# One row block ahead of the last filter load, and the gate products moved behind the kv transforms

## The chip, the cores and the metric

The kernel runs on one core of one Trainium2 chip. A time is the device time of one execution in microseconds (us). The engines are TensorE (PE; its weight loads are listed apart as PEld), VectorE (DVE), ScalarE (ACT), GpSimd (POOL) and SyncE (SP), which issues most of the DMAs. Each engine works through its own instructions in the order in which they were written.

## The reference

Two mixers share one input `x = A_q` (2048 rows, D = 640, bf16), and a gate per row mixes them:

```python
g = sigmoid((x * gate_w).sum(-1))
kv = causal_shift_conv(k, shift_k) * v            # 4 taps
a = x * (causal_long_conv(kv, ssm_k) + kv * ssm_D) # by FFT, length 2S
h = layernorm(x)
b = (gelu(h^T @ w1 + b1) @ w2 + b2)^T             # MLP over the 2048 rows, F = 1536
return g * a + (1 - g) * b
```

## The kernel before, in words

**The convolution.** The FFT is done as matrix products with a table of sines and cosines (`FTB`), after a split of the rows by position modulo 4. The filter `ssm_k` is loaded in five pieces: three for its first half (`SSM0`, line 765) and two for its second (`SSM1`). Each 128-column block is turned by TensorE (`transp`, line 838; evacuated by ScalarE as `wT`), then transformed (`fwd`, `fwd_even`, evacuated as `C`), then combined on VectorE (`mixing`, line 889). K is shifted by small matmuls against `KF` (`kv`, line 1003), multiplied by v, and transformed in the same way; the second half of that product is `kv1`, which lies at `E_base`. `KT`, the turned k, lies there too and is dead by then. VectorE multiplies the transformed parts (`cross`, line 1178; `product`, line 1138), with some sums left to accumulating DMAs from the POOL queue, recombines them (`invmix`), and TensorE transforms back (`inverse`, line 1209).

**The MLP.** The rows (`X`, four blocks of 512 rows, `x_load`, line 737) get their statistics on VectorE (`ln_tile`, line 913), a power on GpSimd (`ln_scale`), and are normalised in place (`ln_apply`). The first MLP product is called m1 (twelve column tiles `ft`, Gelu on ScalarE into `GT`), the second m2 (sixteen tiles). Both are cut into groups of eight matmuls.

**The gate.** The row sum of `X * gate_w` is taken from the normalised rows: VectorE writes a product of two tiles into a buffer `gq`, and ScalarE sums each tile by a copy with an accumulator (`gsum`, lines 1078 to 1085; sixteen of them in `gacc`). `gws` is the sum of the gate's weights. From these `gth`, then a tanh, then `gg`, `omg` and `c2` follow (lines 1087 to 1093). `gq` has two buffers, in space that is later `q_hi`.

**What sets the order.** Every operation is first recorded, with its engine, a duration from a formula, a priority (its place in the program, or a given one: `prio=0` first, MLP groups last) and what it depends on by overlapping memory. Then a list scheduler (`_Sched.run`, line 384) plays this on a clock of its own: each engine takes, whenever it is free, the ready operation with the lowest priority number. A DMA is booked as its bytes over `rate` (365 unless given) behind all earlier DMAs, and lands 2.0 later. At most three convolution tiles and two MLP tiles are in PSUM at once. The instructions are written out in the order that comes out of this. So an edit of a rate, which changes no instruction, can change the order of all engines; an edit of an address changes what has to wait for what.

The MLP groups have the largest priority numbers: in the planner's list they stand wherever TensorE would otherwise have nothing to do.

The lines of the gate and of the loads:

```python
SSM0 = ((0, 1), (1, 3), (3, 5))
...
for a, b in SSM0:
    ssm_load(0, a, b)
for hk in range(4):
    x_load(hk)
```

Of the kernel before, what the change touches and what calls it, by code (L numbers as in the profile page):

```python
# [9 lines left out]
BF16 = mybir.dt.bfloat16  # L10
F32 = mybir.dt.float32
I32 = mybir.dt.int32
ACT = mybir.ActivationFunctionType
# [497 lines left out]
def _build(nc, A_q, A_k, A_v, A_shift_k, A_ssm_k, A_ssm_D, B_x, B_w1, B_b1, B_w2, B_b2, gate_w, out):  # L511
    Bsz, S, D = A_q.shape
# [9 lines left out]
    with ExitStack() as es:  # L522
# [4 lines left out]
        for i in range(4):  # L527
            h = es.enter_context(nc.psum_tensor(f"pp{i}", [128, 1024], F32))
# [7 lines left out]
        def alloc(name, shape, dtype, at=None):  # L536
            size = mybir.dt.size(dtype)
            for s_ in shape[1:]:
                size *= s_
            if at is None:  # L540
                off = cur[0]
                cur[0] = (off + size + 63) // 64 * 64
            else:
                off = at
            assert off % 4 == 0 and off + size <= top, f"SBUF overflow {name}: {off}+{size} > {top}"
            h = nc.alloc_sbuf_tensor_at(name, list(shape), dtype, offset=off)
            T.reg_sbuf(h, off)
# [21 lines left out]
        gacc = alloc("gacc", [128, 16], F32)  # L569
        gws = alloc("gws", [128, 1], F32)  # L570
# [7 lines left out]
        X = alloc("X", [128, 4, 4, D], BF16)  # L578
# [4 lines left out]
        E_base = cur[0]  # L583
# [2 lines left out]
        dif = alloc("dif", [128, 128], I32, at=base_of(SS) + 64 + 1024)  # L586
        dif2 = alloc("dif2", [128, 32], I32, at=base_of(SS) + 64 + 1536)
        KT = [alloc(f"KT{i}", [128, NG, KTW], BF16) for i in range(2)]
        gq = [alloc(f"gq{i}", [128, 2, D], BF16, at=base_of(Drow) + 5120 + 2560 * i) for i in range(2)]
        ssm = alloc("ssm", [128, ND, S], BF16, at=base_of(C[3]))  # L590
        wT = alloc("wT", [128, 4, 4, D], BF16, at=base_of(C[2]))
        vkv0 = alloc("vkv0", [128, 2, 4, D], BF16, at=base_of(C[3]))
# [25 lines left out]
        def act_dur(n, nap=0):  # L618
            return n / 1200.0 + 0.09 + 0.05 * nap

        def tt(eng, o, a, b, op, mode=2, prio=None, xr=()):
            n = n_of(o)
            d = dve_dur(n, mode) if eng == "DVE" else n / 600.0 + 0.17
            rd = [a, b] + list(xr)
            o_ = SC.add(eng, d, lambda s: T.op(eng, lambda e: e.tensor_tensor(o, a, b, op), rd, [o]),  # L625
                        rd, [o], prio=prio, name="tt")
            o_.lock = True
            return o_
# [23 lines left out]
        def act(o, i, func, bias=None, scale=None, acc=None, vt=None, prio=None, name="act"):  # L652
            kw = {}
            rr = []
            nap = 0
            for k_, v_ in (("bias", bias), ("scale", scale)):
                if v_ is not None:
                    kw[k_] = v_
                    if isinstance(v_, bass.AP):
                        rr.append(v_)  # L660
                        nap += 1
            ww = [o]
            if acc is not None:
                kw["accum_out"] = acc
                ww.append(acc)

            def emit(s):
                src = i(s) if vt is not None else i
                return T.op("ACT", lambda e: e.activation(o, src, func, **kw), rr + [src], ww)  # L669
            return SC.add("ACT", act_dur(n_of(o), nap), emit, rr if vt is not None else rr + [i], ww, prio=prio, vt=vt, name=name)  # L670
# [16 lines left out]
        def mms(vt, items, prio=None, name="mm"):  # L687
            dur = sum(max(n_of(r) / 2400.0 + 0.0025, 0.056) for _, _, r, _, _ in items)
            rd = []
            for _, l, r, _, _ in items:  # L690
                rd += [l, r]

            def emit(s):
                fv = T.cnt["PE"] + 1
                for k_, (o, l, r, st, sp) in enumerate(items):
                    T.mm(o(s), l, r, st, sp, fv, k_ == len(items) - 1)
            return SC.add("PE", dur, emit, rd, [], prio=prio, vt=vt, name=name)
# [4 lines left out]
        def dma(o, i, nbytes, stream="SP", prio=None, sem=None, rate=365.0, chain=False, **kw):  # L702
            if sem is None:
                sem = f"d{ndma[0]}"
                ndma[0] += 1
            if sem not in T.dma_sems:
                T.add_dma_sem(sem, es.enter_context(nc.semaphore(f"s_{sem}")))
            rd = [i] + ([o] if kw.get("accum") else [])
            o_ = SC.add(stream, nbytes / rate / 1000.0, lambda s: T.dma({"QA": "ACT"}.get(stream, stream), o, i, sem, **kw), rd, [o], prio=prio, lat=-1.0, name="dma")
            if chain:  # L710
                if last[0] is not None:
                    o_.after.add(last[0])
                last[0] = o_
# [11 lines left out]
        def chk(ci):  # L725
            return lambda s: s[:, ci * 512:ci * 512 + 320]

        def ssm_load(h, a, b):
            dma(ssm[:, a:b, 1024 * h:1024 * h + 1024], dr(A_ssm_k, 128 * S * a + 1024 * h, [[S, 128], [128 * S, b - a], [1, 1024]]), 128 * (b - a) * 2048, chain=True)

        def row8(t, hk):
            return dr(t, (1024 * (hk // 2) + 4 * (hk % 2)) * D, [[8 * D, 128], [1, 4 * D]])
# [2 lines left out]
            return 16 + 128 * (1 - hk % 2)  # L735

        def x_load(hk):
            dma(X[:, hk, :, :], dr(A_q, 512 * hk * D, [[4 * D, 128], [1, 4 * D]]), 128 * 5120, chain=True)

        def w1_load(c, hk):  # L740
            dma(ring[c % 2][:, 4 * hk:4 * hk + 4, :], dr(B_w1, 512 * hk * F + 512 * c, [[4 * F, 128], [F, 4], [1, 512]]), 128 * 4096, chain=True)
# [20 lines left out]
        def small(o, i, nbytes, stream, **kw):  # L762
            dma(o, i, nbytes, stream=stream, **kw)

        SSM0 = ((0, 1), (1, 3), (3, 5))
        SSM1 = ((0, 2), (2, 5))
        small(Drow[:, :], dr(A_ssm_D, 0, [[0, 1], [1, D]]), 1280, "QA")
        small(rows[0:20, 0, 0:128], dr(A_shift_k, 0, [[128, 20], [1, 128]]), 5120, "QA")
        for a, b in SSM0:
            ssm_load(0, a, b)  # L770
        for hk in range(4):
            x_load(hk)
        small(rows[0:4, 1, :], dr(B_b2, 0, [[512, 4], [1, 512]]), 4096, "SP", chain=True)
        small(rows[0:12, 2, 0:128], dr(B_b1, 0, [[128, 12], [1, 128]]), 3072, "SP", chain=True)
        for a, b in SSM1:
            ssm_load(1, a, b)
# [280 lines left out]
        for ft in range(FT):  # L1057
            if ft == 4:
                for hk in range(4):
                    w1_load(2, hk)  # L1060
            if ft == 9:
                for p in range(4):
                    gil = act(V(FTB, 1024 * p, [[1, 2], [256, 4], [2, 128]]), V(GTB, 1024 * p, [[512, 2], [128, 4], [1, 128]]), ACT.Copy, prio=10 ** 5, name="gil")
                    gil.after.add(g_)
            vt = _VT("mlp")
            r = ring[(ft // 4) % 2]
            col = 128 * (ft % 4)
            for hk in range(4):
                items = []
                for p in range(4):  # L1070
                    for ci in range(2):
                        items.append((chk(ci), r[:, 4 * hk + p, col:col + 128], X[:, hk, p, 320 * ci:320 * ci + 320],
                                      hk == 0 and p == 0, hk == 3 and p == 3))
                mms(vt, items, prio=10 ** 6 + 4 * ft + hk, name="m1")
            g_ = act(GT[:, ft, :].rearrange("p (a b) -> p a b", a=2), two, ACT.Gelu_apprx_tanh, bias=cc[:, 16 + ft:17 + ft], vt=vt, prio=0, name="gelu")
            if ft == 0:
                act(gq[1][:, 0, :], gwb[:, :], ACT.Copy, acc=gws[:, :], name="gws").after.add(g_)
            if ft in (1, 3, 5, 7):
                hk = ft // 2
                for a in range(2):  # L1080
                    gb = gq[a]
                    tt("DVE", gb[:, :, :], X[:, hk, 2 * a:2 * a + 2, :], V(gwb, 0, [[0, 2], [1, D]]), ALU.mult)
                    for b in range(2):
                        t = 4 * hk + 2 * a + b
                        act(gb[:, b, :], gb[:, b, :], ACT.Copy, acc=gacc[:, t:t + 1], name="gsum")

        tt("DVE", gth[:, :], sd[:, :], gacc[:, :], ALU.mult, mode=1, prio=0)
        ts("DVE", gpre[:, :], mv[:, :, 0], gws[:, 0:1], None, ALU.mult, mode=1)
# [221 lines left out]
```

## Time and profile before

| | us |
|---|---|
| median of 4 runs | 184.74 (184.35 to 185.58) |
| the profiled execution | 184.35 |
| its span, first to last instruction | 182.6 |
| PE busy | 172.7 |
| DVE busy | 171.7 |
| ACT busy | 117.4 |
| POOL busy | 39.1 |

The profile is one execution. A line of the timeline gives start, duration, engine, line, operation, what it writes and reads, and in brackets how long the engine was idle before it and what released it. In the list of waits the columns are the total, how many times, and the longest. Almost all operations pass through helpers, so most of them share a line (L625 is every elementwise product of VectorE, L669 every ScalarE activation, L293 every matmul); tile names tell them apart. Tile numbers are left out: `C` is four arrays, and `ssm`, `wT`, `vkv` and `SS` are other names with spaces of their own. The clock of TensorE was 1.0 throughout.

### The profile page before, as it was taken

What the parts mean: (1) busy time and instruction counts of PE and PEld (TensorE: products, weight loads), DVE (VectorE), ACT (ScalarE), POOL (GpSimd) and SP (SyncE); (2) the same over time, 40 slices, a digit from 0 to 9 for tenths busy, and PEclk for the clock granted to TensorE, in tenths of its full rate; (3) what the DMA queues carried; (4) which work ended last, traced back from release to release, by engine and by line L of the source; (5) the groups of instructions that cost most, each with busy time, mean ns of one, the idle gap of its engine ahead of it and who ended that gap; (6) DMA issues with size and microseconds to landing.
All of it is one profiled execution on the core that took longest, in us unless ns stands there. A gap on an engine that the chain in (4) does not pass through costs nothing.

```text
span 182.6 us, 3317 instructions
## 1 busy us (share of the span) xinstructions
PE 172.7 (95%) x1373; PEld 127.0 (70%) x1374; DVE 171.7 (94%) x203; ACT 117.4 (64%) x176; POOL 39.1 (21%) x42
## 2 busy tenths in 40 slices
PE   7978998889999999999999999999999999999991
PEld 2644584676777777776777778888888886678670
DVE  7799895999999999999998999999999979999975
ACT  5799988899989978159999931321313213761660
POOL 4069604000000055000510210303443000054000
PEclk9999999999999999999999999999999999999999
DMA  5999999999999989997499969799999997369584
GB/s 156 407 408 370 390 251 238 316 418 199 193 259 280 193 169 242 229 230 168 138 245 260 251 152 353 142 233 344 202 194 273 220 209 204 132 104 232 95 286 148
DMA packets 38542, 43.51 MB, mean 238 GB/s; under 512 B 15867, under 2 KB 31360, under 8 KB 38528
## 3 DMA queue, kind: packets, MB, share of 16 engines
q1 hardware_dynamic: 33296, 32.16, 59.2%
q0 software_dynamic: 5200, 11.14, 34.2%
q8 instruction: 11, 0.18, 0.4%
q10 hardware_dynamic: 32, 0.01, 0.0%
q14 instruction: 3, 0.02, 0.0%
HBM read 25.87 MB, written 2.62 MB: 156 GB/s over the span
## 4 chain that ended last, share of the span: by engine, by line
PE 38%; DVE 30%; ACT 18%; DMA 9%; issue 3%; DVEq 0%; SPq 0%
PE pp L293 38%; DVE C L625 21%; DMA C<-SS 7%; ACT C L669 5%; ACT gq L669 5%; DVE tm L625 4%; DMA ssm<-in_A_ssm_k_dram 3%; ACT FTB L669 2%; DVE q_hi L625 2%; ACT wT L669 2%; ACT GT L669 2%; DVE gq L625 1%; DVE SS L625 1%; ACT L669 1%; ACT ksh L669 1%
## 5 line engine op out<-in xcount | busy, mean ns | idle before, releaser
L625 DVE TENSOR_TENSOR C<-C 128x2560 bf16<-128x2560 bf16 (+2 forms) x37 | 54.7, 1522 | 1.7 <-DMA C<-SS 1.2
L293 PE MATMUL pp<-X,ring 128*128 128x320 bf16 x384 | 55.1, 299 | 0.0
L293 PE MATMUL pp<-GT,W 128*128 128x320 bf16 x384 | 52.8, 299 | 0.0
L293 PEld LDWEIGHTS pp<-GT,W 128*128 128x128 bf16 x384 | 43.4, 113 | 8.8 <-ACT cgb L669 0.2
L293 PEld LDWEIGHTS pp<-X,ring 128*128 128x128 bf16 x384 | 37.3, 98 | 14.4
L669 ACT ACTIVATE C<-pp 128x640 bf16<-128x640 f32 x64 | 40.1, 725 | 5.0 <-PE pp L293 5.0
L669 ACT ACTIVATE O<-pp,c,omg 128x640 bf16<-128x640 f32 x15 | 13.3, 886 | 33.8 <-PE pp L293 33.8
L262 POOL DMA_DIRECT2D C<-C x8 | 10.9, 1609 | 46.7 <-DVE C L625 46.3
L293 PE MATMUL pp<-wT,FTB 128*128 128x320 bf16 x112 | 17.8, 301 | 1.6 <-ACT C L669 1.4
L669 ACT ACTIVATE cgb<-pp,gg 128x640 bf16<-128x640 f32 x16 | 12.7, 794 | 8.9 <-PE pp L293 8.9
L293 PEld LDWEIGHTS pp<-wT,FTB 128*128 128x128 bf16 x112 | 9.5, 97 | 8.8 <-ACT C L669 5.2
L669 ACT ACTIVATE GT<-pp,cc 128x640 bf16<-128x640 f32 x12 | 9.4, 786 | 8.3 <-PE pp L293 8.2
L919 DVE BATCH_NORM_STATS2 stats<-X 128x6 f32<-128x320 bf16 x32 | 13.7, 465 | 0.9 <-DMA X<-in_A_q_dram 0.9
L625 DVE TENSOR_TENSOR tm<-C,C 128x2560 bf16<-128x2560 bf16 (+1 forms) x7 | 14.3, 2057 | 0.0
L293 PE MATMUL pp<-C,FTB 128*128 128x320 bf16 x96 | 13.6, 299 | 0.5 <-DVE C L625 0.5
L262 POOL DMA_DIRECT2D C<-q_hi x6 | 5.9, 978 | 31.2 <-DVE C L625 16.2
L293 PEld LDWEIGHTS pp<-C,FTB 128*128 128x128 bf16 x96 | 9.0, 98 | 4.7 <-issue 0.7
L669 ACT ACTIVATE gq<-gq 128x640 bf16<-128x640 bf16 x16 | 11.6, 732 | 0.3 <-DVE gq L625 0.3
L625 DVE TENSOR_TENSOR SS<-C 128x2560 bf16<-128x2560 bf16 x8 | 11.7, 1487 | 0.1
L625 DVE TENSOR_TENSOR C<-tm 128x2560 bf16<-128x2560 bf16 (+1 forms) x9 | 10.6, 1192 | 0.1
L669 ACT ACTIVATE wT<-pp 128x1024 bf16<-128x1024 f32 x10 | 9.5, 1034 | 1.2 <-PE pp L293 1.2
L293 PE MATMUL pp<-KF,KT 128*128 128x128 bf16 (+1 forms) x160 | 9.0, 213 | 1.2 <-ACT GT L669 1.1
(73 smaller groups left out, 186.9 us busy)
## 6 DMA issues: line engine op xcount, KB each, us to landing
ring<-in_B_w_dram SPq DMA_DIRECT2D x12, 512.0 KB, 11.0
W<-in_B_w_dram SPq DMA_DIRECT2D x12, 512.0 KB, 7.2
C<-C POOLq DMA_DIRECT2D x8, 640.0 KB, 11.8
X<-in_A_q_dram SPq DMA_DIRECT2D x4, 640.0 KB, 8.2
kn<-in_A_k_dram SPq DMA_DIRECT2D x4, 640.0 KB, 9.4
out_dram<-O SPq DMA_DIRECT2D x7, 320.0 KB, 3.0
C<-SS POOLq DMA_DIRECT2D x3, 640.0 KB, 12.3
ssm<-in_A_ssm_k_dram SPq DMA_DIRECT2D x3, 512.0 KB, 5.5
```

The source lines that it names most:

```text
L262: ins = engobj.dma_start(out_ap, in_ap, accum_op=ALU.add, max_dma_last_dim=2560)
L293: ins = self.nc.tensor.matmul(ps_ap, lhsT=lhsT, rhs=rhs, start=start, stop=stop, skip_group_check=True)
L625: o_ = SC.add(eng, d, lambda s: T.op(eng, lambda e: e.tensor_tensor(o, a, b, op), rd, [o]), rd, [o], prio=prio, name="tt")
L669: return T.op("ACT", lambda e: e.activation(o, src, func, **kw), rr + [src], ww)
L919: ops.append(SC.add("DVE", 0.38, (lambda o, i: lambda s: T.op("DVE", lambda e: e.bn_stats(o, i), [i], [o]))(o, i), [i], [o]))
```

## The change

First, the loads: the first X block is issued between the second and the third filter piece, where before all three filter pieces went first. The booked rates are other ones: 262 for the first filter piece, 195 for the next two, 385 for the second half, 410 for X.

Second, the gate: the products use four buffers at `E_base`, the space of `kv1` (and of the dead `KT`), where before there were two in the later `q_hi`. So they have to wait until the transforms of `kv1` have read it. The scratch row of `gws` gets its own name, `gqd`. All eight products are recorded at `ft == 0`, where before two each were recorded at `ft` 1, 3, 5 and 7; in the program they stand behind the transforms of kv and ahead of `cross`, as before.

```diff
-        gq = [alloc(f"gq{i}", [128, 2, D], BF16, at=base_of(Drow) + 5120 + 2560 * i) for i in range(2)]
+        gqd = alloc("gqd", [128, D], BF16, at=base_of(Drow) + 5120)
+        gq = [alloc(f"gq{i}", [128, 2, D], BF16, at=E_base + 2560 * i) for i in range(4)]
...
         def ssm_load(h, a, b):
-            dma(ssm[...], dr(A_ssm_k, ...), 128 * (b - a) * 2048, chain=True)
+            dma(ssm[...], dr(A_ssm_k, ...), 128 * (b - a) * 2048, chain=True, rate=(262.0 if a == 0 else 195.0) if h == 0 else 385.0)
...
         def x_load(hk):
-            dma(X[:, hk, :, :], dr(A_q, ...), 128 * 5120, chain=True)
+            dma(X[:, hk, :, :], dr(A_q, ...), 128 * 5120, chain=True, rate=410.0)
...
-        for a, b in SSM0:
+        for a, b in SSM0[:2]:
             ssm_load(0, a, b)
-        for hk in range(4):
+        x_load(0)
+        ssm_load(0, *SSM0[2])
+        for hk in range(1, 4):
             x_load(hk)
...
             if ft == 0:
-                act(gq[1][:, 0, :], gwb[:, :], ACT.Copy, acc=gws[:, :], name="gws").after.add(g_)
-            if ft in (1, 3, 5, 7):
-                hk = ft // 2
-                for a in range(2):
-                    gb = gq[a]
+                act(gqd[:, :], gwb[:, :], ACT.Copy, acc=gws[:, :], name="gws").after.add(g_)
+            if ft == 0:
+                for t in range(0, 16, 2):
+                    hk, a = t // 4, t // 2 % 2
+                    gb = gq[t // 2 % 4]
                     tt("DVE", gb[:, :, :], X[:, hk, 2 * a:2 * a + 2, :], V(gwb, 0, [[0, 2], [1, D]]), ALU.mult)
                     for b in range(2):
-                        t = 4 * hk + 2 * a + b
-                        act(gb[:, b, :], gb[:, b, :], ACT.Copy, acc=gacc[:, t:t + 1], name="gsum")
+                        act(gb[:, b, :], gb[:, b, :], ACT.Copy, acc=gacc[:, t + b:t + b + 1], name="gsum")
```

More of the change, by code (lines that the diff above doesn't have):

```diff
@@ L728, in ssm_load @@
         def ssm_load(h, a, b):
-            dma(ssm[:, a:b, 1024 * h:1024 * h + 1024], dr(A_ssm_k, 128 * S * a + 1024 * h, [[S, 128], [128 * S, b - a], [1, 1024]]), 128 * (b - a) * 2048, chain=True)
+            dma(ssm[:, a:b, 1024 * h:1024 * h + 1024], dr(A_ssm_k, 128 * S * a + 1024 * h, [[S, 128], [128 * S, b - a], [1, 1024]]), 128 * (b - a) * 2048, chain=True, rate=(262.0 if a == 0 else 195.0) if h == 0 else 385.0)
         def row8(t, hk):
@@ L737, in x_load @@
         def x_load(hk):
-            dma(X[:, hk, :, :], dr(A_q, 512 * hk * D, [[4 * D, 128], [1, 4 * D]]), 128 * 5120, chain=True)
+            dma(X[:, hk, :, :], dr(A_q, 512 * hk * D, [[4 * D, 128], [1, 4 * D]]), 128 * 5120, chain=True, rate=410.0)
         def w1_load(c, hk):
```

## The prediction

> **What bounds the kernel now.** I read the page's busy shares first, then the table of stretches, then the waits, then the timeline at each wait.
>
> ```profile
> PE 172.7 (95%) x1373; PEld 127.0 (70%) x1374; DVE 171.7 (94%) x203; ACT 117.4 (64%) x176; POOL 39.1 (21%) x42
> ```
>
> TensorE and VectorE are both nearly full: of 182.6 us PE is idle for 9.9, DVE for 10.9. An edit that removes no instruction can only move these idle pieces. The table of stretches says where they lie (busy time out of the stretch's length: PE, PEld, DVE, ACT, POOL).
>
> ```profile
> 28.00:30.00 2.00, 1.98 (x15) 1.18 (x13) 0.92 (x4) 1.12 (x2) 0.87 (x2) 1.00 1.18 245
> 30.00:32.00 2.00, 1.15 (x6) 0.44 (x7) 0.94 (x3) 2.00 (x4) 1.24 (x2) 1.00 1.14 215
> 36.00:38.50 2.50, 1.35 (x24) 1.20 (x24) 2.43 (x4) 2.49 (x5) 0.00 (x0) 1.00 1.00 414
> 38.50:80.00 41.50, 41.45 (x378) 30.57 (x379) 41.00 (x29) 32.87 (x50) 5.10 (x4) 1.00 1.05 233
> 80.00:153.00 73.00, 72.76 (x536) 57.05 (x533) 70.85 (x61) 37.13 (x64) 14.40 (x13) 1.00 0.96 226
> ```
>
> From 38.5 to 153 PE loses 0.05 + 0.24 us: the MLP matmuls fill every hole. What PE loses, it loses before 38.5 (0.85 at 30 to 32, 1.15 at 36 to 38.5) and after 178. DVE loses 0.5 + 2.15 us there, and its waits name it:
>
> ```profile
> DVE X L640 <- POOL rstd L625: 2.7, 2, 2.1
> DVE C L625 <- DMA C<-SS: 1.2, 1, 1.2
> DVE stats L919 <- DMA X<-in_A_q_dram: 0.9, 1, 0.9
> DVE gth L625 <- ACT gq L669: 0.5, 1, 0.5
> ```
>
> The last two are what the diff touches. The row that ties both engines together is on PE's timeline:
>
> ```profile
> 153.22 0.97 PE L293 MATMUL pp<-C,FTB 128*128 128x320 bf16 x6 [0.46 <-DVE C L625]
> ```
>
> At 153.22 the inverse transforms start, and PE had to wait 0.46 us for VectorE. So VectorE's chain, from the second normalisation at 31.07 to 153.2, sets the end; PE is only 0.46 us behind. After 153.22 PE is full until 178.5. A microsecond gained on PE alone before 153 is given back there; one lost on DVE is lost in full.
>
> [...] the trace has 1.28 us at 34.90, ahead of the first Gelu. The planner's costs know no such load. [...] The trace has 0.72 for one gsum, but with its accumulator read 0.72 from start to start; the planner books 640/1200 + 0.09 = 0.62. [...] 410 to 430 GB/s from 6 to 11 us.
>
> **Part 1, the loads.** Nothing is added; one 640 KB X block goes ahead of the last 512 KB filter load. From the issues and their times to landing: ssm (1,3) is in at 5.89 (PE's wait ends there); ssm (3,5) is issued at 1.64 and takes 5.5, so 7.2; X block 0 is issued at 2.20 and takes 6.6, so 8.8. At about 400 GB/s the 640 KB take 1.6 us: X block 0 lands at 7.5, the filter piece at 8.8, all later blocks as before.
> VectorE: it waited 0.89 us until 8.80 for X. In the new order it is free at 7.91 and X is there, so the statistics, and the last angle product behind which POOL's four KF products queue (8.13 us, first start 10.77), begin 0.89 earlier. rstd, the first normalised rows (20.93) and, after the same 2.11 us wait for POOL, the second eight (31.07) come at 20.04 and 30.18. Gain so far: 0.89.
> ScalarE: the new rates change the planner's order. It now believes that the second and third filter pieces land later (5.79 and 10.09 on its clock, 4.26 and 5.71 before). By its priorities two sines then go ahead of wT evacuations: the third sine before wT1 (a near tie on its clock, 6.583 against 6.589), the fourth before wT3. The trace had those sines at 11.91 and 16.59, 1.03 us each, with PE waiting. The work is the same. wT4 then ends at about 13.2 instead of 11.9, but the 16 C evacuations (0.6 each) have no sine among them. I get their end at 23.6 to 24.5 against 23.58, the spread being whether PE, which now meets the first MLP group inside this phase, waits for X (about 0.45 us) in the middle of it. Cost on PE at this point: +0.1 to +0.9. After it there is one more MLP group already done or in reach, and the holes at 30 to 32 and 36 to 38.5 (2.0 us) are partly filled: I take 0.5 gained. Net on PE to 38.5: -0.4, from -1.2 to +0.6.
> The catch: VectorE after 31.07 does a few products and then needs the last C evacuation of the second filter half. In the trace that evacuation stands behind the table load and the first Gelu (34.90 + 1.28, Gelu to 36.99, C to 37.59), and DVE resumed at 37.61. These ScalarE times hang on the filter chain, not on X. With VectorE at 36.7 there, it waits for nearly the same 37.5. So of the 0.89 us I keep 0.1 as likeliest, up to 0.89 if the planner, seeing that evacuation late, puts another product in between. I take -0.3.
> The K transposes move too: the planner has K landing 1.8 us later, so the two DVE permutes at 23.07 and 24.92 go behind the last normalised rows, some 0.8 us later; their transposes on SP (23.92, 6.92 us for both), and the v and k loads queued behind them at 30.89, shift by as much. KT landed at 32.7 for a first use at 35.02, v (5.2 us) at 36.1 for 39.93: hidden. Without that cover it would be 0.8 us on VectorE.
>
> **Part 2, the gate products.** Eight products on DVE (0.73 from start to start) and sixteen gsums on ACT (0.72) stay. They now write the space of kv1, so the first must wait for the last kv1 matmul (84.68 + 0.71 = 85.4); in the trace two products ran at 81.30 and 84.84, ahead of that. VectorE will not idle: the first cross product (1.40) is ready and takes the slots of those two (1.47). The first gate product comes at about 85.5, just when kv1 is dead; two C[3] differences (2.80) go ahead of the next, so three more products come from 88.4 to 90.6 and, by the four buffers, the last near 95. Cost on DVE so far: nothing, covered by the cross products, 16 pieces of 0.73 to 1.40; if these were not ready, 1.4 us.
> The sum over the rows (gth) then waits for ScalarE. From the second gate product (ends about 89.9) 14 gsums and two Gelus (0.68) remain: 14 x 0.72 + 2 x 0.68 + 0.1 = 11.5, so 101.4. By the planner's 0.62 they would be 14 x 0.1 = 1.4 us sooner, and it puts gth at the first slot after that; VectorE reaches gth at about 100.2 and stands for 1.2 us, against 0.53 before. Bounds: the slot's rounding, up to one 1.40 us product, may swallow all of it (-0.5 against before) or it may be 1.9 (+1.4). I take +0.7. Behind gth on DVE stand the cross products, the C[3] sums, and so all up to 153. The gates' own end has slack: c2 at 103.44 for a first user at 111.57.
>
> **Sum.** VectorE at 153.2: -0.3 + 0.7 = +0.4; PE arrives 0.4 earlier and waits longer for it. The rest is unchanged. The profiled execution took 184.35 (span 182.6 and 1.75 around it), so 184.75; the median of the runs shown lies 0.39 above the profiled one, so 185.1 in its terms. A measurement of this kernel can tell about 0.5% (0.92 us) from no change, so this counts as the same.
>
> **Rivals.**
> Faster: VectorE keeps its lead of 0.89 at 37.6 and gth waits no longer than 0.53. For it: the hole before gth has room for 1.40 us of rounding, and PE has 2.0 us of early idle to give. Against: ScalarE's table load ends where it ended. Then -0.9 at 153.2, and the 0.46 us wait shrinks with it: 183.8, at best 183.3.
> Slower: one MLP group changes sides. The planner's list has the inverse's first input at 149.52 on its clock, between group ends at 149.20 and 150.28. I get PE's useful work 0.19 late on that clock, as the W transforms start 2.7 later and most of it is caught up by 39. From a lag of 0.33 on, one MLP group less runs before the inverse and one more after, where PE has no hole: 8 matmuls, 1.09 us from start to start. With VectorE's +0.4: 186.2. For it: 0.14 us decides. Against: the same rounding can give a group back.
> The change does not do what it says: the filter piece behind X lands much later than 8.8 (the new rates would have it past 10), ScalarE starves before wT3, and the filter chain, with everything hung on it at 37.6, is 0.5 to 1 us late: 185.8.
>
> **How the numbers follow.** Forecast 0.45 (its own range 184.1 to 185.6), faster 0.22, a group moved 0.23, the late filter piece 0.10. The last two together make slower, 0.33. For 8 in 10 the range takes in the faster case down to 183.7 and the moved group with the longer gth wait up to 186.7.
>
> **What would show it.** DVE's wait for X at 8.8 gone, statistics from 7.9; a DVE wait for ACT C near 37; gate products after 85; gth's wait for gq over 1 us; PE's wait for DVE at the first inverse matmul grown from 0.46 to about 1.2. I am wrong if that wait shrinks, if gth waits under 0.5, or if the MLP matmuls left after the inverse starts (56 now) are another number.

## The result, and the profile after

The kernel after has a median of 185.95 us (183.73 to 187.82, 43 runs); the kernel before, measured beside it, 185.46 (183.79 to 187.46, 64 runs). The ratio is 0.9984, with a 95% interval of 0.9963 to 1.0005: by the bound of 0.5%, no change. In terms of the 184.74 of the front page this is 184.4. The medians are over all runs, while the ratio leaves out those over 1.5% above the fastest of their kernel (19 of 43 after, 6 of 64 before), which is why the two don't agree in sign.

The profiled execution took 185.93 us, its span is 183.8, so it is 1.2 us longer than that of the kernel before. Its loads came late, as the experiments will show. First the page's busy shares and its row of TensorE's clock in 40 slices:

```profile
PE 174.6 (95%) x1373; PEld 128.9 (70%) x1374; DVE 171.8 (93%) x203; ACT 117.6 (64%) x176; POOL 43.5 (24%) x42
...
PEclk9958999999999999999999999999999999999999
```

The instruction counts are the same, VectorE's work too (171.8 against 171.7). TensorE is busy 1.9 us longer for the same 1373 matmuls, and the clock row has a dip in the third and fourth slices, 9 to 18 us, that the kernel before doesn't have. Now the same stretches as before (PE, PEld, DVE, ACT, POOL busy; clock; DMA share; GB/s):

```profile
30.00:32.00 2.00, 1.84 (x14) 1.09 (x12) 0.94 (x3) 1.12 (x2) 1.24 (x2) 1.00 0.83 159
36.00:38.50 2.50, 1.39 (x11) 0.80 (x10) 2.50 (x3) 2.49 (x4) 2.50 (x1) 1.00 1.02 395
38.50:80.00 41.50, 41.44 (x403) 31.20 (x402) 40.16 (x30) 34.50 (x53) 5.67 (x5) 1.00 1.03 251
80.00:153.00 73.00, 73.00 (x537) 57.10 (x535) 70.19 (x59) 37.09 (x64) 14.40 (x13) 1.00 0.97 219
```

TensorE's hole at 30 to 32 is nearly filled (0.16 instead of 0.85 us), the one at 36 to 38.5 is not (1.11 instead of 1.15). VectorE now loses 1.34 us from 38.5 to 80 (0.5 before) and 2.81 from 80 to 153 (2.15 before). Its list of waits (total, times, longest) gives the names:

```profile
DVE X L641 <- POOL rstd L626: 2.7, 2, 2.1
DVE gth L626 <- ACT gq L670: 1.2, 1, 1.2
DVE stats L922 <- DMA X<-in_A_q_dram: 0.9, 1, 0.9
DVE C L626 <- DMA C<-SS: 0.8, 1, 0.8
DVE C L626 <- ACT C L670: 0.5, 1, 0.5
DVE vkv L626 <- ACT ksh L670: 0.3, 1, 0.3
```

The wait at `gth` has grown from 0.5 to 1.2. A wait for the filter's copies (`C`) and one for `ksh`, both for ScalarE, are there near 40 us. The wait for X has not gone: in this execution X block 0 landed at 8.80. TensorE's timeline from the inverse on:

```profile
154.65 4.51 PE L293 MATMUL pp<-C,FTB 128*128 128x320 bf16 x32 [1.65 <-DVE C L626]
159.00 2.34 PE L293 MATMUL pp<-GT,W 128*128 128x320 bf16 x16
...
165.61 3.45 PE L293 MATMUL pp<-GT,W 128*128 128x320 bf16 x24
...
177.68 3.45 PE L293 MATMUL pp<-GT,W 128*128 128x320 bf16 x24
```

The inverse starts at 154.65 instead of 153.22, and TensorE has waited 1.65 us for VectorE. After it 16 + 24 + 24 = 64 MLP matmuls are left, where before there were 56.

**VectorE's ledger.** TensorE's wait of 1.65 us says that VectorE comes last at the inverse. Where VectorE lost the time is found by adding its idle time up to there. Length less busy time (the third figure behind the length) from 5 us to the inverse, first of the kernel before:

```profile
5.00:42.00 37.00, 32.77 (x314) 22.42 (x313) 33.14 (x81) 33.95 (x47) 12.67 (x11) 1.00 1.06 352
42.00:90.00 48.00, 48.00 (x404) 34.59 (x402) 47.59 (x37) 38.61 (x66) 7.29 (x6) 1.00 0.97 202
90.00:153.22 63.22, 62.76 (x464) 50.10 (x462) 61.07 (x52) 27.90 (x46) 12.21 (x12) 1.00 1.01 239
```

and of the kernel after:

```profile
5.00:42.00 37.00, 33.37 (x297) 23.21 (x297) 32.46 (x80) 32.55 (x45) 17.03 (x11) 0.91 1.01 337
42.00:90.00 48.00, 47.95 (x414) 34.94 (x411) 47.49 (x35) 37.01 (x59) 6.30 (x5) 1.00 0.97 217
90.00:154.65 64.65, 63.00 (x464) 50.20 (x463) 61.84 (x53) 31.16 (x55) 13.20 (x12) 1.00 1.01 232
```

Before: 3.86 + 0.41 + 2.15 = 6.42 us idle. After: 4.54 + 0.51 + 2.81 = 7.86. The difference, 1.44, is that of the two starts of the inverse, 1.43, as it must be where VectorE comes last and has the same work before it. (TensorE's idle time up to the same point grows by 0.64 only, from 4.69 to 5.33.) 0.68 of the loss lies before 42 us, where the new load order should have brought a gain.

### The profile page after: what moved, and what is told of

It is laid out like the page before. It is cut to its first block, busy times and chain, and to the rows that moved or that the text cites. A ratio compares the mean times of both kernels' runs of the same rounds, so it can differ in the third digit from the quotient of the medians.

```text
span 183.8 us, 3318 instructions
## 1 busy us (share of the span) xinstructions
PE 174.6 (95%) x1373; PEld 128.9 (70%) x1374; DVE 171.8 (93%) x203; ACT 117.6 (64%) x176; POOL 43.5 (24%) x42
## 4 chain that ended last, share of the span: by engine, by line
PE 51%; DVE 18%; ACT 15%; DMA 11%; issue 3%; SPq 1%
PE pp L293 51%; DVE C L626 11%; DMA C<-SS 7%; ACT gq L670 6%; DMA ssm<-in_A_ssm_k_dram 4%; DVE tm L626 4%; ACT C L670 4%; DVE q_hi L626 2%; ACT ksh L670 2%; ACT GT L670 2%; ACT FTB L670 1%; DVE SS L626 1%; SPq L267 1%; ACT L670 1%; DVE O L682 0%
## 5 line engine op out<-in xcount | busy, mean ns | idle before, releaser
L670 ACT ACTIVATE C<-pp 128x640 bf16<-128x640 f32 x64 | 40.7, 715 | 7.1 <-PE pp L293 7.0
L293 PEld LDWEIGHTS pp<-wT,FTB 128*128 128x128 bf16 x112 | 10.6, 101 | 8.1 <-ACT C L670 3.1
L262 POOL DMA_DIRECT2D O<-q_hi x4 | 4.8, 1324 | 25.0 <-DVE q_hi L626 25.0
```

The costliest lines, as they stand in the source:

```text
L262: ins = engobj.dma_start(out_ap, in_ap, accum_op=ALU.add, max_dma_last_dim=2560)
L293: ins = self.nc.tensor.matmul(ps_ap, lhsT=lhsT, rhs=rhs, start=start, stop=stop, skip_group_check=True)
```

## The experiments

My theory at the outset went by the first profile and no longer by the prediction: X lands at 8.8 again, so that the load order gains nothing, and each part lengthens VectorE's chain by about 0.7 us. The rival was that this profile had been disturbed early on. The first four kernels take the change apart; the other eight follow a cause that these four brought up. Each was measured beside the kernel before on the same chip.

| kernel | median us | ratio to before, 95% | second half's `wT` copies begin | wait at `gth` | inverse begins |
|---|---|---|---|---|---|
| before (first profile) | | | 24.17 | 0.53 | 153.22 |
| after (first profile) | 185.95 | 0.9984 (0.9963 to 1.0005) | 26.03 | 1.23 | 154.65 |
| change_again | 185.16 | 0.9963 (0.993 to 0.9997) | 26.61 | 1.23 | 155.55 |
| loads_alone | 185.37 | 0.9985 (0.9951 to 1.002) | 25.77 | none | 153.38 |
| gates_alone | 185.09 | 1.0011 (0.998 to 1.0042) | 24.10 | 0.74 | 153.05 |
| gsum_cost | 184.60 | 0.9943 (0.9911 to 0.9975) | 24.35 | 0.15 | 152.64 |
| keep_pace | 186.53 | 1.0078 (1.005 to 1.0106) | 27.16 | 1.2 | 155.80 |
| keep_pace_gsum | 185.66 | 1.0007 (0.9979 to 1.0035) | 27.04 | 0.2 | 154.78 |
| before_cold | 186.20 | 1.0071 (1.0045 to 1.0097) | 25.59 | 0.5 | 154.52 |
| gsum_on_before | 185.28 | 0.9987 (0.996 to 1.0015) | 24.14 | none | 153.25 |
| fill_pause | 184.28 | 0.996 (0.9939 to 0.9982) | 25.36 | 1.2 | 154.14 |
| fill_gsum | 183.19 | 0.989 (0.9851 to 0.9929) | 24.31 | 0.2 | 151.91 |
| gates_gsum | 185.23 | 1.0005 (0.9971 to 1.0038) | 24.81 | none | 153.39 |
| loads_fill_gsum | 182.90 | 0.9878 (0.9835 to 0.9921) | 24.55 | none | 152.34 |

Medians are over all runs; the kernel before had 184.95 in the first four (75 runs), 184.75 in the next four (69), 185.04 in the next three (35) and 185.09 beside the last (11). The last three columns are of the one profiled execution; the fourth says when the filter chain on ScalarE is done with the first half. "None" at `gth` means that VectorE found it ready (in loads_alone, gsum_on_before and loads_fill_gsum it then waits 0.7 to 0.8 at `gg`, for ScalarE's tanh of it).

**The change again, and its two parts.** change_again is the kernel after, unchanged. loads_alone takes the first half of the diff, the load order and the booked rates, with the gate as before. gates_alone takes the other half, the gate products, with the loads as before.

> The changed kernel once more, unaltered. My theory (both parts only lengthen VectorE's chain, by about 0.7 us each, and the end absorbs one MLP group): X block 0 lands near 8.8 again and not at 7.5, the last filter piece of the first half after 10; VectorE waits for ScalarE near 39.5 and near 42 (0.9 together) and for the row sums 1.2 us; TensorE waits over 1 us at the first inverse matmul. Rival (the first profile was disturbed by a dip of the TensorE clock early on): with the clock at 1.0 the waits near 39.5 and 42 are gone and X lands at 7.5.

> Part 1 alone (order and rates of the loads; the gate as before). My theory: no gain at the first statistics (8.8), waits of about 0.5 and 0.3 us for ScalarE near 39.5 and 42, TensorE's wait at the first inverse matmul near 1.7 us, because one MLP group less is planned ahead of it and VectorE is about 0.7 later; time against the kernel before 0 to +0.7 us. Rival A (the planner's own shorter schedule is real): 0.4 us faster. Rival B (nothing of it reaches the end): within 0.2 us.

> Part 2 alone (gate products in the space of kv1, four buffers; loads and rates as before). My theory: no gate product before kv1 is read (85); the wait before the row sums grows from 0.53 to between 0.8 and 1.3 us; TensorE's wait at the first inverse matmul grows from 0.46 by as much; time +0.3 to +0.8 us. Rival (gates are off the chain): the wait at the inverse stays within 0.2 of 0.46 and the time within 0.2 us.

Neither part is told from no change (0.9985 and 1.0011). My theory missed for both. For gates_alone I had 0.3 to 0.8 us more and a longer wait of TensorE at the inverse; the wait at `gth` grew by 0.21 only, and TensorE waited 0.39 there, where before it was 0.46. In change_again and in loads_alone X was no longer late: VectorE's statistics start at 7.83 and 7.82 (8.86 in gates_alone). So the landing at 8.80 in the first profile was that execution's own; there the loads came about 1.1 us late. But the rival fails too, since the lead from X is gone all the same. VectorE's timeline of change_again near 40 us shows one place where it goes:

```profile
40.06 2.23 DVE L626 TENSOR_TENSOR C<-C 128x1280 bf16<-128x1280 bf16 x2 [0.91 <-ACT C L670]
42.62 1.49 DVE L626 TENSOR_TENSOR vkv<-ksh,vkv 128x2560 bf16<-128x2560 bf16 x1 [0.34 <-ACT ksh L670]
```

1.25 us of waits for ScalarE's copies, and 0.47 more at 35.52. The filter chain is late: the second half's `wT` copies begin at 26.61, 2.4 us later than before. In loads_alone the waits are 0.63 and 0.34 us and the copies begin 1.6 later.

**The planner is told what a gsum costs.** The planner books 0.62 us for a `gsum`; in the trace each is an activation and, 0.62 us after its start, an instruction that reads the accumulator, and from one `gsum` to the next it is 0.72. gsum_cost corrects that in the kernel after, which moves VectorE's `gth` to a later place in the order:

```diff
-  act(gb[:, b, :], gb[:, b, :], ACT.Copy, acc=gacc[:, t + b:t + b + 1], name="gsum")
+  act(gb[:, b, :], gb[:, b, :], ACT.Copy, acc=gacc[:, t + b:t + b + 1], name="gsum").dur += 0.1
```

> The changed kernel with 0.1 us more booked for each gsum (what its accumulator read takes), so that the planner puts the row sums' product later. My theory: the wait before it falls from 1.2 to under 0.3 us, TensorE's wait at the first inverse matmul falls by about as much (0.9), and the time against the changed kernel by 0.5 to 1.0 us. Rival (that wait is made up for later, by the wait for the accumulating DMA ahead of the last recombination): VectorE arrives at the inverse within 0.2 us of where it was, and the time stays.

The ratio is 0.9943, though its interval overlaps that of change_again, and the wait at `gth` is down to 0.15:

```profile
101.58 0.17 DVE L626 TENSOR_TENSOR gth<-sd,gacc 128x16 f32<-128x16 f32 x1 [0.15 <-ACT gq L670]
```

But the inverse is 2.9 us earlier than in change_again, and that wait is shorter by only 1.08. By the ledgers 1.75 us of VectorE's idle time has gone before 42 us, where the two programs are the same: no wait for `C` at 38, and `wT` copies from 24.35 instead of 26.61. After 90 us only 0.59 has gone, since 0.73 of the 1.08 comes back as a longer wait for the sum by DMA ahead of the last recombination (1.94 instead of 1.21). TensorE's timeline of change_again from 6 us on, three of its rows:

```profile
6.26 0.61 PE L293 MATMUL pp<-zz 128*128 128x512 bf16 x1 [1.12 <-ACT wT L670]
...
7.01 1.07 PE L293 MATMUL pp<-ident,ssm 128*128 128x128 bf16 x8
...
14.52 3.13 PE L293 MATMUL pp<-wT,FTB 128*128 128x320 bf16 x16
```

and the same three of gsum_cost:

```profile
6.19 0.39 PE L293 MATMUL pp<-zz 128*128 128x512 bf16 x1 [1.11 <-ACT wT L670]
...
6.67 0.71 PE L293 MATMUL pp<-ident,ssm 128*128 128x128 bf16 x8
...
12.87 2.47 PE L293 MATMUL pp<-wT,FTB 128*128 128x320 bf16 x16
```

The same instructions take 1.3 to 1.6 times as long in change_again: 0.61 for 0.39 (a filler matmul on zeros, `zz`), 1.07 for 0.71 (eight transposes), 3.13 for 2.47 (16 filter matmuls). This lasts until 14 to 18 us. The profiled execution of change_again, at 188.68 us, is one of its longest: in it the inverse's first 12 matmuls, behind TensorE's wait of 2.00 us, take 2.89 us, where the first 17 take 2.47 in keep_pace, and the clock row has a dip there (two slices of 7 and 8). But loads_alone, whose execution of 185.07 is an ordinary one, has the same early stretch:

```profile
6.26 0.61 PE L293 MATMUL pp<-zz 128*128 128x512 bf16 x1 [1.12 <-ACT wT L669]
...
7.02 1.07 PE L293 MATMUL pp<-ident,ssm 128*128 128x128 bf16 x8
```

In change_again and loads_alone the page's clock row reads 9 through all of this stretch, so the pace has to be read from the durations. They show two paces, the slow one and the full one. The kernel before begins at the slow pace: its first eight transposes, at 4.07, take 1.08 us, and all from 5.94 on 0.71 to 0.72. Between the two lies a factor of two: three fillers in a row take 1.49 us at the slow pace (keep_pace_gsum, below), where one takes 0.61, and 0.82 at the full one (before), where one takes 0.38, so that from start to start it is (1.49 - 0.61) / 2 = 0.44 us against (0.82 - 0.38) / 2 = 0.22.

The slow pace takes the lead from X at an earlier place too. TensorE's small transposes of `shift_k` come later with it, and so does ScalarE's copy of them (`cw`), on which POOL's KF products hang. loads_alone, then gsum_cost:

```profile
10.06 0.29 ACT L669 ACTIVATE cw<-pp 128x140 bf16<-128x140 f32 x1 [0.86 <-PE pp L293]
...
9.02 0.28 ACT L670 ACTIVATE cw<-pp 128x140 bf16<-128x140 f32 x1
```

POOL begins these products at 10.43 and at 9.78. Behind them stands its `rstd`, so VectorE begins the second normalisation at 30.72 in loads_alone and at 30.07 in gsum_cost (31.07 before). Two thirds of the lead are lost here, the rest in the waits near 40 us.

What differs early between the kernels is TensorE's idle time. In the kernel before it waits 0.28 us between 4.9 and 6. With the new rates the planner gives the second filter transpose the same PSUM buffer as the first, since by its clock the filter piece lands late enough; so TensorE stands from 5.1 to 6.2 until ScalarE has copied the first one out. gsum_cost has the same pause, of 1.11, and yet the full pace behind it. The new theory, called "pace", is a guess from these durations: behind this pause TensorE stays at the slow pace in some executions, or falls back to it; the filter's copies then come 1.4 to 2.3 us late, and VectorE pays near 40 us. Its rival, "swallowed": the copies may come late, but VectorE's chain doesn't feel it.

**A first remedy, and the fillers taken out.** keep_pace gives the second transpose another PSUM buffer and three fillers ahead of it instead of one. keep_pace_gsum adds the `gsum` cost.

```diff
-                    op.vt.slot = nfree.pop(0)
+                    op.vt.slot = nfree.pop(op.vt.nth if op.vt.nth < len(nfree) else 0)
...
-        SPIN = (6, 1, 1, 1, 1)
+        SPIN = (6, 3, 1, 1, 1)
...
         def transp(h, db):
             vt = _VT("cv")
+            vt.nth = int((h, db) == (0, 1))
```

before_cold goes the other way: the kernel before, with the fillers behind the first six taken out.

```diff
-        SPIN = (6, 1, 1, 1, 1)
+        SPIN = (6, 0, 0, 0, 0)
...
-                    m_ = mms(vt, (spin(3) if lead else []) + items, name=name)
+                    m_ = mms(vt, (spin(0) if lead else []) + items, name=name)
```

> The kernel before without its filler matmuls after the first six (no filler ahead of the other four transposes and none ahead of the filter's first transform); nothing else changes, and the planner's order is the same. Theory 'pace': TensorE is now too seldom busy between 5 and 12 us, and in many or all executions its matmuls take 1.5 times as long there (16 filter matmuls above 3 us); the filter's copies on ScalarE end 0.5 to 1.5 us later than 23.58, and the time rises by 0.3 to 1.2 us (ratio 1.002 to 1.007), with executions in two groups. Rival 'swallowed': VectorE's chain sets the end and does not hang on these copies; within 0.15% of the kernel before.

> The kernel after, with its early pause on TensorE filled: the second filter transpose gets another PSUM buffer than the first, so that it no longer waits for the first one's copy, and has three filler matmuls ahead of it instead of one. Theory 'pace': in the kernel after, TensorE is idle from 5.1 to 6.2 us, and in many executions its matmuls then take 1.5 times as long until 14 to 17 us (filler 0.61 instead of 0.38 us, 16 filter matmuls 3.1 instead of 2.47). With the pause filled they run at 0.38 and 2.47 in every execution, the first filter half's 16 copies end near 24.5 instead of 25.9 to 26.7, VectorE waits less than 0.3 us for the copy near 38 to 40, and the time falls by 0.4 to 1.0 us against the kernel after: 0.991 to 0.995 of the kernel before. Rival 'swallowed': the copies come earlier but the table load and the first Gelu hold the last one as before, so the time stays within 0.3 us of the kernel after: 0.996 to 0.999.

> The same filled pause, together with the planner's gsum cost raised by 0.1 us (gsum_cost). Theory 'pace': the two gains add, since one lies before 40 us and the other near 100: ratio to the kernel before 0.988 to 0.992, gth waits under 0.3 us and the copy near 38 under 0.3 us. Rival: gsum_cost had its 0.9943 from a fast start alone; then this is 0.993 to 0.996.

before_cold is slower, 1.0071, as "pace" has it. It has less work for TensorE than the kernel before and the same order. The kernel before, 24 filter matmuls:

```profile
11.71 3.79 PE L293 MATMUL pp<-wT,FTB 128*128 128x320 bf16 x24
```

and before_cold, 23 of them, and the inverse:

```profile
11.94 4.99 PE L293 MATMUL pp<-wT,FTB 128*128 128x320 bf16 x23 [0.47 <-ACT wT L669]
...
154.52 4.51 PE L293 MATMUL pp<-C,FTB 128*128 128x320 bf16 x32 [0.38 <-DVE C L625]
```

They take 1.2 us longer, the `wT` copies begin 1.42 later, the inverse 1.30 later, the span is 1.3 longer: a late filter chain arrives at the end nearly whole. (X landed 0.57 later too in this execution, but VectorE waits 0.93 us for the filter's copy behind that, so the copy is what holds it.) "Swallowed" is out. I had expected two groups of executions: the ten whose mean granted clock is 0.98 or 0.99, which shows a dip, span 182.8 to 184.2 us, the eleven at 1.0 span 184.2 to 185.1 (one at 0.97 spans 185.4), as if these had not reached full pace before the slow stretch, which no profile shows. The longest pause in before_cold's profile ahead of the slow stretch is 0.79 us, before 6.12.

keep_pace missed. It was to be faster and is slower than the kernel after, 1.0078. Its timeline shows that the pause was not filled but moved:

```profile
10.79 0.61 PE L293 MATMUL pp<-zz 128*128 128x512 bf16 x1 [1.29 <-ACT wT L671]
...
11.54 1.07 PE L293 MATMUL pp<-ident,ssm 128*128 128x128 bf16 x8
...
15.34 2.80 PE L293 MATMUL pp<-wT,FTB 128*128 128x320 bf16 x16
```

The second and third transposes are now done early and at full pace (0.71), but ScalarE, which has two sines ahead of their copies, is no earlier; so TensorE stands 1.29 us before the fourth (1.84 in keep_pace_gsum), and from there the slow durations are back until 18 us. The slow stretch comes later. (In keep_pace's profiled execution the loads were about 1.1 us late as well.) keep_pace_gsum missed likewise, 1.0007 where I had 0.988 to 0.992. But it shows what the pace is worth inside one program, where only the execution differs: by the mean granted clock of its 22 executions, the four at 1.0 span 181.6 to 182.8 us, the nine at 0.99 182.6 to 183.8, and the nine at 0.98 183.6 to 185.6. This speaks for "pace" and against the remedy.

**gsum on the kernel before.** The same cost edit without the change, for the worth of that wait alone.

> The kernel before with only the planner's gsum cost raised by 0.1 us; loads and gate products stay where they were. It measures the worth of the gth wait alone. Theory: gth's wait of 0.53 us goes, VectorE comes to the inverse up to 0.5 us earlier, where TensorE is only 0.46 us behind, so the time falls by 0.1 to 0.5 us: ratio 0.997 to 0.9995. Rival: gsum_cost's whole gain over the kernel after came from the gth wait (1.23 to 0.15), in which case a wait's length is passed on in full and this gives 0.997. A second rival: the order that the new cost brings costs as much as the wait; 1.000 or more.

0.9987, not told from no change. The wait of 0.53 at `gth` is gone, but 0.7 us of waiting stands at `gg` behind it, and the inverse starts at 153.25. So gsum_cost's gain is not to be had without the rest.

**The pauses filled in place.** fill_pause leaves the order and all buffers of the kernel after alone and puts fillers in a PSUM buffer of their own into the pauses that TensorE has anyway: three behind the first transpose, two behind the third, two behind the fifth.

```diff
-                    op.vt.slot = nfree.pop(0)
+                    op.vt.slot = nfree.pop(-1 if op.name == "fill" else 0)
...
+        FILL = {(0, 0): 3, (0, 2): 2, (0, 4): 2}
...
+        def fill(k, ahead):
+            f_ = mms(_VT("mlp"), spin(k), prio=-2, name="fill")
+            f_.dur = 0.01
+            f_.after.add(ahead)
...
         def transp(h, db):
...
+            if (h, db) in FILL:
+                fill(FILL[(h, db)], m_)
```

fill_gsum adds the `gsum` cost to it; gates_gsum is part 2 alone with the `gsum` cost.

> The kernel after with three small filler groups for TensorE in a PSUM buffer that nothing else uses by then: three filler matmuls behind the first filter transpose, two behind the third, two behind the fifth. No other operation changes its order or its buffer. Theory 'pace': the fillers run in pauses that TensorE has anyway (1.1, 0.5 and 0.8 us), TensorE stays at full pace from about 5 us on (filler 0.38 us, 16 filter matmuls 2.47), the 16 copies of the first filter half end at 24.4 to 24.6 (25.9 and 26.7 in the slow-paced executions), the inverse starts 0.8 to 1.4 us earlier than in those (below 154), and the time is 0.5 to 1.2 us below the kernel after: ratio to the kernel before 0.991 to 0.995. Rival: the copies come earlier but VectorE, held at gth and near 38 us, gives it back; then the ratio stays at 0.996 to 1.000.

> The same fillers with the planner's gsum cost raised by 0.1 us. Theory 'pace': gsum_cost's profile was of a full-paced start and spans 181.8 us, while over a third of its executions were 1.5 us longer; with the fillers all are near 181.5 to 182.2, so ratio 0.987 to 0.992. Rival: the longer executions have another cause; then the ratio is that of gsum_cost, 0.993 to 0.996.

> Part 2 alone, with the planner's gsum cost raised by 0.1 us and the loads as in the kernel before. If part 2 is worth something once its wait at gth (0.74 in gates_alone) is gone: VectorE reaches the inverse 0.3 to 0.5 us earlier and the ratio is 0.996 to 0.998. If part 2 is worth nothing by itself, since TensorE is 0.4 us behind at the inverse: 0.998 to 1.001, as gsum_on_before (0.9987). In neither case is 0.994 in reach, which would need part 1.

fill_gsum has 0.989, the best so far. In its profiled execution TensorE is at full pace from 4 us on (0.72 for the first eight transposes), already ahead of the first new filler, and it stays there behind the fillers. Its timeline:

```profile
4.63 0.81 PE L293 MATMUL pp<-zz 128*128 128x512 bf16 x3
5.91 0.39 PE L293 MATMUL pp<-zz 128*128 128x512 bf16 x1 [0.47 <-ACT wT L670]
...
12.82 2.47 PE L293 MATMUL pp<-wT,FTB 128*128 128x320 bf16 x16
...
151.91 4.51 PE L293 MATMUL pp<-C,FTB 128*128 128x320 bf16 x32 [0.60 <-DVE C L626]
```

and VectorE's ledger (again the third busy time):

```profile
5.00:42.00 37.00, 33.88 (x322) 23.44 (x321) 33.98 (x82) 33.72 (x46) 17.18 (x11) 1.00 1.01 337
42.00:90.00 48.00, 48.00 (x403) 34.88 (x401) 47.57 (x36) 37.03 (x62) 6.30 (x5) 1.00 1.01 227
90.00:151.91 61.91, 61.31 (x453) 48.98 (x451) 60.08 (x51) 29.47 (x51) 13.20 (x12) 1.00 1.01 234
```

3.02 + 0.43 + 1.83 = 5.28 us idle, 1.14 less than in the kernel before, with the inverse 1.31 earlier. 0.84 of it is before 42 us: the lead from X, 0.9, has been kept.

fill_pause has the same early program. TensorE begins it at the slow pace (1.07 for the first eight transposes) and is at 0.71 from 7.55 on; 16 filter matmuls take 2.47 and the filler 0.38, though its profiled execution had the loads about 1.1 us late again (TensorE waits for the second filter piece until 7.55), so its copies come 0.9 later than I had written. What tells more is the spread: the spans of its 22 runs lie between 181.9 and 183.3 us, those of change_again's 23 between 181.8 and 186.5, with eleven up to 182.4 and the others from 183.0 on. The long executions have gone and the short ones are no shorter. That is what "pace" expects, though no profile shows that each long execution was a slow start; a late load and the dip at the inverse (above) lengthen some too. By the medians of all executions against the kernel before, the fillers bring 0.5% (change_again 1.001, fill_pause 0.996) and 0.8% (gsum_cost 0.998, fill_gsum 0.990). I had put it at 0.991 to 0.995; it is 0.996, at the border of the rival's range, because the wait at `gth` is still 1.2. The edits of the two fill kernels differ in the `gsum` cost alone. Their waits at `gth` differ by 1.08 us (1.24 and 0.16), VectorE's idle time from 90 us to the inverse by 0.97 (2.80 and 1.83), and their medians by 1.09. So this wait is paid nearly in full here.

gates_gsum, 1.0005, is no faster than part 2 alone. Its wait at `gth` is gone and TensorE doesn't wait for VectorE at the inverse any more (153.39), so TensorE is then the one that comes last, in an execution whose X landed at 9.74.

**Part 1 without part 2.** The last kernel has the load order, the fillers and the `gsum` cost, and the gate products in their old place.

> Part 1 alone (the gate products where they were before) with the same fillers and the raised gsum cost. It shows what part 2 is worth once TensorE keeps its pace and the gth wait is gone. If part 2 is worth nothing: the same as fill_gsum, ratio 0.987 to 0.992, spans 181 to 182. If fill_gsum's gain needs part 2: ratio 0.993 to 0.997. loads_alone's faster executions spanned 181.3 to 181.9, so the first is the likelier.

```profile
152.34 4.51 PE L293 MATMUL pp<-C,FTB 128*128 128x320 bf16 x32 [0.93 <-DVE C L625]
```

182.90 us, 0.9878: the fastest of all, and not told from fill_gsum by the intervals. Both kernels of the case are beaten, by a version that has only the first half of the change, with the fillers and the `gsum` cost. No run puts these two into the kernel before, which has pauses of 0.48 and 0.65 us at 9 to 11 us itself, so what part 1 adds to them is not shown. Part 2 is worth nothing here that could be measured, and the longer wait at `gth` that comes with it costs about 1 us until the `gsum` cost is put right (fill_pause against fill_gsum).

## Why the prediction was right, and where it was not

The time was right: 185.1 was forecast, as no change, with a range of 183.7 to 186.7; the ratio makes it 184.4. By its steps:

- **What sets the end** ("VectorE's chain ... sets the end", "one lost on DVE is lost in full"): right. TensorE waits for VectorE at the inverse in before, after and fill_gsum, the ledgers agree with the starts of the inverse to 0.2 us, and the fill pair shows it for one single wait. "In full" is too strong: of the shorter wait at `gth` in gsum_cost two thirds came back at a later wait.
- **X earlier.** Statistics at 7.91 were forecast: 7.83 and 7.82 in change_again and loads_alone. The filter piece behind X was to land at 8.8; in those executions it lands at 9.0 to 9.1. Normalised rows at 20.04 and 30.18 were forecast: 19.94 and 30.07 in gsum_cost, but 20.59 and 30.72 in those two, where POOL was held up by `cw`. In the profile shown first, with its late loads, X came at 8.80 and that piece at 10.1, so the marker "wait for X gone" fails there and holds in the others. The rival of a late filter piece is what that one execution shows, though by late loads and not by the change.
- **ScalarE's order.** "I get their end at 23.6 to 24.5": 24.47 in gsum_cost and 24.42 in fill_gsum, but 25.9 in loads_alone and 26.7 in change_again. This is the step that failed. It took TensorE's matmuls at the durations of the kernel before and asked only in which order they come; the edit also opened a pause of 1.1 us at 5.1, and in part of the executions the same matmuls then take 1.3 to 1.6 times as long. The pause could have been foreseen from the planner's list; its effect on the pace could not be seen in the trace of before.
- **The catch.** "of the 0.89 us I keep 0.1 as likeliest": neither value is the rule. In after, change_again and loads_alone VectorE waits 0.54 to 0.91 for `C` and 0.34 for `ksh` near 40 us, and the lead is gone; in gsum_cost, fill_gsum and loads_fill_gsum there is no wait for `C` and 0.15 to 0.34 for `ksh`, and it is kept. The table load and the first Gelu, which were held to fix the time, move with the filter chain: the load stands at 33.85 in gsum_cost and at 36.10 in change_again (34.90 before). The -0.3 lies between two cases, and is not what either does.
- **The gates.** Products after 85 (the first at 87.81, 85.5 was forecast), a wait of 1.2 at `gth` (1.23 measured), +0.7 against before: right in size and in its cause, a `gsum` that the planner books too short. But two shifts cancel in it. ScalarE begins its sums only at 89.61, behind copies of `kv1`'s transforms, so all sixteen and not fourteen still lie ahead and `gth` starts at 102.61 instead of 101.4; and VectorE comes to it at 101.38 instead of 100.2. (The working has a slip as well: a first product at 85.5 and two differences of 2.80 put the next at about 89.1, not 88.4; the 89.9 that it goes on with fits the 89.1.) The fill pair puts the worth of the part that the planner's cost takes away at 1.09.
- **The sum.** VectorE at the inverse +0.4, TensorE waiting about 1.2: +1.43 and 1.65 in the first profile. The sum was too small by the filter chain's delay and the X that came late there. That the executions with a full pace make up for it in the median is likely, and not shown: only one execution of each run has a profile.
- **One group moved.** The prediction calls itself wrong if the 56 MLP matmuls left become another number. They are 64, so by that mark it was wrong. But the price that the rival put on it, 1.09 us "where PE has no hole", was not paid: from the start of the inverse to the end of the span it is 29.4 us before and 29.2 after. Before, TensorE ended at 178.51 and VectorE's last operation at 180.45; after, they end at 181.13 and 181.72, and VectorE's last operation waits 0.17 for TensorE. The eight matmuls went into that gap of 1.9 us at the end.
- **Faster rival** (VectorE keeps its lead and `gth` waits no longer): 183.8 forecast. This is gsum_cost and fill_gsum, at ratios of 0.9943 and 0.989, so 183.7 and 182.7 in the same terms. Its mechanism was right; it needs the pace and the `gsum` cost, which the change doesn't bring.

The total was right in part by luck: the step that failed, TensorE's matmuls held to keep their durations, makes two kinds of execution, and -0.3 for the lead is what neither does. As far as the runs show, "no change" comes out of a gain and a loss that both are about 1 us: a lead from X that is kept or lost with TensorE's pace, and a longer wait at `gth` from the gate products.

What stays open: what makes TensorE slow in the first 18 us. That the pauses have to do with it is inferred from the slow durations that follow some of them and from what the fillers do; no run shows why the same pause has the slow pace behind it in one execution (1.12 us in change_again) and the full one in another (1.11 in gsum_cost). Nor is it settled whether the kernel before, whose executions span 181.8 to 186.0, has slow starts too; its one profile has none, nor have those of gates_alone, gsum_on_before and gates_gsum, which begin with the same program, and the filled kernels are 2 us faster in the median where the profiles differ by 1.2 to 1.5.

## What to carry to other kernels

Fix the start before weighing the middle: where a change opens a pause on TensorE in the first 15 us, compare the durations of identical matmuls between two profiles before comparing the order of anything, and try a few fillers in the pause. Find the engine that another one waits for at a common point, and add up its idle time to there: the differences say where it lost, but a wait that has gone can come back at a later one. An operation whose cost the planner understates turns into a wait of the engine that was scheduled behind it, which a corrected cost can remove without touching the kernel's work.

## What the runs showed of the hardware

- A pause of 1.1 us at 5 us (loads_alone, change_again), or of 0.79 with the fillers gone (before_cold), came with slow durations on TensorE for up to 10 us more (matmuls of 128x512: 0.61 instead of 0.38 us; 24 of 128x320: 1.2 us more). It does so in part of the executions: gsum_cost's profile has the same pause, of 1.11, at full pace (a filler of 0.39 behind it). Pauses of 1.29 (keep_pace) and 1.84 us (keep_pace_gsum) had slow durations behind them too (0.61 for the filler); one of 0.75 us had not (fill_pause, 0.71 for eight transposes).
- A pause of 2.00 us at the inverse was followed by 12 matmuls in 2.89 us (change_again); behind pauses of 1.64 to 1.71 us at the same place the first 17 took 2.47 (keep_pace) and 32 took 4.51 (after, keep_pace, fill_pause).
- The clock row shows a dip where TensorE had been at full pace and fell back (two slices of 5 to 8; eight transposes 0.71 us at 7.17 and 1.07 at 10.17 in after, 0.70 at 8.53 and 1.07 at 11.54 in keep_pace, 0.71 at 6.92 and 1.07 at 9.41 in before_cold), but none where it had not yet reached it (1.07 at 4.07 and still at 12.36 in loads_alone and change_again, the row at 9 all the while).
- On ScalarE a sum over 640 elements takes a second instruction, which reads the accumulator: it starts 0.62 us after the activation, and the next activation 0.10 later (the gate's sums in after).
- Loads from one queue land up to 1.7 us later in some executions than in others: the second filter piece ends TensorE's wait at 5.84 (gates_alone), 5.94 (before), 6.12 (before_cold), 6.57 (gates_gsum), 7.17 (after), 7.51 (keep_pace) and 7.55 us (fill_pause), and in fill_gsum it was there by 6.38.
